# Linear attention with per-channel decay, feed-forward and experts: attention's output made transposed in 32- and 64-column groups of the matmul array, reciprocal decays made by a backward scan

## The chip, the core and the metric

The kernel runs on one core of one Trainium2 chip. The metric is the device time of one launch in microseconds (us); lower is better. Engines are named as in the profile: PE (matmuls), PEld (loads of a matmul's stationary operand), DVE, ACT, POOL, SP (issues most transfers).

## The reference

Three steps follow each other. The first is a recurrence over 768 positions, for 4 batches and 8 heads of 48 channels:

```python
for t in range(S):
    cur = np.einsum('bhd,bhe->bhde', u[None] * kt, vt)
    y[:, :, t] = np.einsum('bhd,bhde->bhe', rt, state + cur)
    state = wt[:, :, :, None] * state + np.einsum('bhd,bhe->bhde', kt, vt)
```

Its output, 3072 tokens by 384, goes through `x @ w_in` (384 to 2048), `max(h, 0) + alpha * min(h, 0)` and `@ w_out` (2048 to 384). The last step routes each token to one of 8 experts (384 to 1024 to 384, relu) by the largest of 8 logits and scales by its probability. All of it is fp32.

## The kernel before

**Stages.** The 3072 tokens are 24 tiles of 128, and 8 blocks of 3 tiles. Attention of tiles 0 to 2 is a prologue. Then the feed-forward step runs block by block, 16 steps of 128 hidden columns each (`p1`, L575, 9 matmuls of 384 columns; `p2`, L602, 9 matmuls of 384 columns). Attention of the next block's tiles is laid between these steps, and so are, in the first block, the conversion of 16 pieces of weights (`wl_stages`, L195, its word operations on DVE) and, one block late, the routing of a finished block (`gate_block`, L462). At the end the expert units run. A product of fp32 numbers in the two feed-forward steps is made from a high and a low part, three matmuls in one pass each. The matmuls of attention are plain fp32: the trace counts two passes for each of them, and one for a transpose.

**One attention tile** (`att_tile`, L265) works on 4 pairs of heads. Channels lie on partitions (0 to 47 the first head of a pair, 64 to 111 the second) and the 128 positions of each pair along the free axis. `scan` (L274) makes the running products of the decays (`ex`, 4 runs of 129). `decay_r` multiplies r by them on POOL. `rec(0)` takes the reciprocal of every fourth product, `rec(1)` fills the three between by multiplying backwards with the decays, `rec(2)` multiplies k; all on DVE. `diag`, `diag_sum` and `diag_v` make `cv`, v scaled by the sum of r, u and k of the position itself. `scores` (L342) makes a 128x128 matrix for each head, on 48 rows of the array, the two heads of a pair on different rows; ACT copies it out and POOL zeroes the part on and above the diagonal. `ktr` and `kv` make the update of the state; `state` adds it on DVE and multiplies by `pm` on POOL; `pm` is made on ACT (`decay`, L336) and has a single buffer. The output is then made in three places:

- `yst` (L398): 4 matmuls, r stationary (128 columns), the state moving (96 columns), into `py`;
- `yav` (L410), in two halves of 4 heads: scores stationary (128 columns), v moving (48 columns), into the same bank;
- `fin` (L422) adds `cv` on DVE into `x`, and `xtr` (L427) transposes `x` in three matmuls into `px`. ACT copies `px` to `xth` (L441), DVE makes `xtl` from the rest (L446). These are the feed-forward step's input, channels on partitions.

**What sets the order.** Tables of slots (`OPS`, and `PRO_OPS`, `PRO_MOVED` for tiles 0 to 2) give each operation of a tile its slot; a feed-forward step is two slots. On PE the order is that of the tables throughout. On DVE, ACT, POOL and SP it is that of the tables in the prologue, and a list scheduler's from there up to the last steps of the feed-forward stage. Each engine works strictly in its order. A tile's `dm` (r, k, decays, channels on partitions) and `tm` (r, k, v, positions on partitions) are loaded by SP, two tiles ahead.

Of the kernel before, what the change touches and what calls it, by code (L numbers as in the profile page):

```python
# [27 lines left out]
PR = 112  # L28
KC = DM // 128
# [44 lines left out]
}  # L74
PRO_NEXT = ("scan", "rec0", "rec1", "k", "r", "rk")
PRO_MOVED = {
# [20 lines left out]
def attention_mlp_moe(ctx, tc, dmaj, tmaj, ub, alpha, w_in, w_out, w_gate, w_gate_b, wexp, out):  # L97
# [23 lines left out]
    def load_tile(i):  # L121
        if i < NB:
            both = wp.tile([128, 1540 + 3 * DM], F32, tag="W", name="both")
            dm, tm = both[:PR, :1540], both[:, 1540:].rearrange("p (c d) -> p c d", c=3)
# [16 lines left out]
    pool.memset(bmask[0:48, :, 0:48], 1.0)  # L141
    pool.memset(bmask[64:112, :, 48:96], 1.0)
# [11 lines left out]
    pool.memset(apat[:, :, 0:1], 1.0)  # L154
    ident = cst.tile([128, 128], F32, name="ident")
# [109 lines left out]
    def att_tile(i, s0):  # L265
# [8 lines left out]
        def scan():  # L274
            dm = dm_t[i]
            ex = ap.tile([PR, NP, 129], F32, tag="ex", name="ex")
            vec.tensor_tensor_scan(
                out=ex.rearrange("p a t -> p (a t)"),
                data0=dm[:, 1024:1540],
                data1=apat.rearrange("p a t -> p (a t)"),  # L280
                initial=0.0,
                op0=ALU.mult,
                op1=ALU.add,
            )
# [3 lines left out]
            cx["v"] = tm_t[i][:, 2, :]  # L288
            cx["rec"] = ap.tile([PR, NP, 128], F32, tag="rec", name="rec", bufs=1)
# [4 lines left out]
        def rec(n):  # L294

            def at4(t, m):
                return t.rearrange("p a (g m) -> p a g m", m=4)[:, :, :, m]

            rc, ex = cx["rec"], cx["ex"][:, :, 1:129]
            if n == 0:  # L300
                vec.reciprocal(out=at4(rc, 3), in_=at4(ex, 3))
            elif n == 1:
                w = dm_t[i][:, 1024:1540].rearrange("p (a t) -> p a t", a=NP)[:, :, 1:129]
                for m in (2, 1, 0):
                    vec.tensor_tensor(out=at4(rc, m), in0=at4(rc, m + 1), in1=at4(w, m + 1), op=ALU.mult)
            else:
                vec.tensor_tensor(out=cx["k"], in0=cx["k"], in1=rc, op=ALU.mult)

        def diag():
            tm = tm_t[i]  # L310
            rk = ap.tile([128, DM], F32, tag="rk", name="rk", bufs=1)
            pool.tensor_tensor(out=rk, in0=tm[:, 0, :], in1=tm[:, 1, :], op=ALU.mult)
            pool.tensor_tensor(out=rk, in0=rk, in1=ub_s, op=ALU.mult)
            cx["rk"] = rk
# [6 lines left out]
        def diag_v():  # L321
            c = cx["c"]
            cv = ap.tile([128, H, D], F32, tag="cv", name="cv", bufs=1)
            if i < NB:
                for h in range(H):
                    act.activation(cv[:, h, :], cx["v"][:, D * h : D * h + D], AF.Copy, scale=c[:, h : h + 1])
            else:
                pool.tensor_tensor(
                    out=cv,
                    in0=cx["v"].rearrange("p (h d) -> p h d", h=H),  # L330
                    in1=c.rearrange("p (h o) -> p h o", o=1).to_broadcast([128, H, D]),
                    op=ALU.mult,
                )
            cx["cv"] = cv
# [63 lines left out]
        def yst():  # L398
            cx["y"] = y_bank("py", [128, DM])
            if not first:  # L400
                for p in range(NP):
                    pe.matmul(
                        cx["y"][:, 96 * p : 96 * p + 96],
                        lhsT=cx["r"][:, p, :],
                        rhs=st_t[i - 1][:, p, :],
                        start=p == 0,
                        stop=False,
                    )

        def yav(g):  # L410
            v = cx["v"]
            for q in range(4):
                h = 4 * g + q
                pe.matmul(
                    cx["y"][:, D * h : D * h + D],
                    lhsT=cx[h % 2][:, h // 2, :],
                    rhs=v[:, D * h : D * h + D],
                    start=first,
                    stop=first or h == H - 1,
                )  # L420

        def fin():  # L422
            x = ap.tile([128, DM], F32, tag="x", name="x", bufs=1)
            vec.tensor_tensor(out=x, in0=cx["y"], in1=cx["cv"].rearrange("p h d -> p (h d)"), op=ALU.add)
            cx["x"] = x

        def xtr():  # L427
# [5 lines left out]
            pa = y_bank("px", [128, KC, 128])  # L433
            for c in range(KC):
                pe.transpose(pa[:, c, :], cx["x"][:, 128 * c : 128 * c + 128], ident)
            cx["px"] = pa
# [6 lines left out]
        def x_low():  # L443
# [5 lines left out]
            "scan": scan, "r": decay_r, "rec0": lambda: rec(0), "rec1": lambda: rec(1), "k": lambda: rec(2),  # L449
            "rk": diag, "c": diag_sum, "cv": diag_v, "sc": scores,  # L450
            "a0": lambda: scores_out(0), "m0": lambda: mask(0), "a1": lambda: scores_out(1), "m1": lambda: mask(1),
            "yst": yst, "yav0": lambda: yav(0), "yav1": lambda: yav(1), "fin": fin, "xtr": xtr, "xh": x_out, "xl": x_low,
# [640 lines left out]
```

## Time and profile before

| what | value |
|---|---|
| runs | 878.28, 880.32, 882.10 us; median 880.32 |
| the profiled execution | 875.71 us, of which span 874.0 us |
| PE busy in the span | 820.5 us (94%) |
| DVE | 645.4 us (74%) |
| ACT | 384.3 us (44%) |
| POOL | 293.4 us (34%) |
| granted TensorE clock, mean | 0.961 of full speed |
| bytes moved | 111.59 MB, mean 128 GB/s |

A busy share is a mean over stages. The first feed-forward matmul starts at 41.8 us, the last piece of weights is converted at about 136 us, the last feed-forward matmuls start at 606 us, and the last matmuls of the experts at 860 us. Busy time by stage is among the rows below. The chain that ended last, as the profile gives it, holds only the last scatter of the output.

### The profile page before, as it was taken

What the parts mean: (1) busy time and instruction counts of PE and PEld (TensorE: products, weight loads), DVE (VectorE), ACT (ScalarE), POOL (GpSimd) and SP (SyncE); (2) the same over time, 40 slices, a digit from 0 to 9 for tenths busy, and PEclk for the clock granted to TensorE, in tenths of its full rate; (3) what the DMA queues carried; (4) which work ended last, traced back from release to release, by engine and by line L of the source; (5) the groups of instructions that cost most, each with busy time, mean ns of one, the idle gap of its engine ahead of it and who ended that gap; (6) DMA issues with size and microseconds to landing.
All of it is one profiled execution on the core that took longest, in us unless ns stands there. A gap on an engine that the chain in (4) does not pass through costs nothing. (4 is left out here: it accounts for less than half of the span.)

```text
span 874.0 us, 14602 instructions
## 1 busy us (share of the span) xinstructions
PE 820.5 (94%) x5453; PEld 796.1 (91%) x5453; DVE 645.4 (74%) x1219; ACT 384.3 (44%) x751; POOL 293.4 (34%) x309
## 2 busy tenths in 40 slices
PE   6878789999799999999999999999999999999994
PEld 4768779999799999999999999999899999999993
DVE  6999898977686996896996983446767576776761
ACT  3545343344133433333333432337355556565641
POOL 5474444233332433343423330122224122232301
PEclk8779888999899999999999999999999999999997
DMA  9625534022212321311312300036456668585830
GB/s 281 203 83 171 193 120 148 29 60 86 59 59 60 87 60 60 86 60 60 86 60 59 87 1 1 28 137 242 147 202 240 224 216 293 204 294 204 275 119 21
DMA packets 30513, 111.59 MB, mean 128 GB/s; under 512 B 8229, under 2 KB 11592, under 8 KB 30440
## 3 DMA queue, kind: packets, MB, share of 16 engines
q1 hardware_dynamic: 26088, 100.38, 35.8%
q0 software_dynamic: 4352, 10.26, 3.2%
q8 instruction: 44, 0.72, 0.3%
q14 instruction: 29, 0.24, 0.1%
HBM read 100.95 MB, written 10.45 MB: 127 GB/s over the span
## 5 line engine op out<-in xcount | busy, mean ns | idle before, releaser
L584 PE MATMUL ph<-xth,wih 128*128 128x384 f32 x384 | 138.1, 360 | 8.4 <-DVE gt L589 5.2
L610 PE MATMUL py<-woh,gh 128*128 128x384 f32 x384 | 138.1, 360 | 1.0 <-ACT gh L595 1.0
L584 PE MATMUL ph<-xth,wil 128*128 128x384 f32 x384 | 132.9, 346 | 6.2 <-DVE wil L229 6.2
L595 ACT CAST gh<-gt 128x384 fp32r<-128x384 f32 x128 | 65.6, 513 | 158.5 <-DVE gt L589 158.5
L610 PE MATMUL py<-woh,gl 128*128 128x384 f32 x384 | 131.4, 342 | 1.4 <-DVE gl L597 1.4
L584 PE MATMUL ph<-xtl,wih 128*128 128x384 f32 x384 | 132.3, 345 | 0.0
L610 PE MATMUL py<-wol,gh 128*128 128x384 f32 x384 | 131.2, 342 | 0.0
L597 DVE TENSOR_TENSOR gl<-gt,gh 128x384 fp32r<-128x384 f32 x128 | 91.9, 718 | 33.3 <-ACT gh L595 31.8
L589 DVE SCALAR_TENSOR_TENSOR gt<-gn,oma_s,ph 128x384 f32<-128x384 f32 x128 | 76.4, 597 | 50.3 <-ACT gn L587 50.1
L587 ACT ACTIVATE gn<-ph 128x384 f32<-128x384 f32 x128 | 62.7, 490 | 113.2 <-PE ph L584 110.1
L815 DVE SCALAR_TENSOR_TENSOR gl<-ph,gh 128x256 fp32r<-128x256 f32 x96 | 40.4, 422 | 73.9 <-ACT gh L813 67.2
L489 DVE SCALAR_TENSOR_TENSOR sink<-x,wgb 128x384 f32<-128x384 f32 x144 | 88.1, 634 | 2.1 <-ACT x L621 1.4
L584 PEld LDWEIGHTS ph<-xth,wih 128*128 128x128 f32 x384 | 74.6, 194 | 10.3 <-DVE gt L589 5.8
L810 PE MATMUL ph<-xh,w1h 128*128 128x256 f32 x288 | 81.5, 283 | 1.2 <-DVE gl L815 1.1
L584 PEld LDWEIGHTS ph<-xth,wil 128*128 128x128 f32 x384 | 74.7, 194 | 7.4 <-DVE wil L229 7.4
L884 POOL DMA_INDIRECT out<-ys,meta x28 | 28.5, 1018 | 156.3 <-ACT ys L881 97.5
L810 PE MATMUL ph<-xl,w1h 128*128 128x256 f32 x288 | 80.8, 281 | 0.0
L810 PE MATMUL ph<-xh,w1l 128*128 128x256 f32 x288 | 80.4, 279 | 0.0
L610 PEld LDWEIGHTS py<-woh,gh 128*128 128x128 f32 x384 | 74.7, 195 | 3.0 <-ACT gh L595 1.3
L610 PEld LDWEIGHTS py<-woh,gl 128*128 128x128 f32 x384 | 74.1, 193 | 2.5 <-DVE gl L597 2.5
L584 PEld LDWEIGHTS ph<-xtl,wih 128*128 128x128 f32 x384 | 74.9, 195 | 0.8 <-DVE xtl L446 0.3
L610 PEld LDWEIGHTS py<-wol,gh 128*128 128x128 f32 x384 | 74.6, 194 | 0.0
(211 smaller groups left out, 1906.4 us busy)
## 6 DMA issues: line engine op xcount, KB each, us to landing
raw<-w SPq DMA_DIRECT2D x64, 768.0 KB
dm<-dmaj SPq DMA_DIRECT2D x21, 673.8 KB
tm<-tmaj SPq DMA_DIRECT2D x21, 576.0 KB
raw<-w_out SPq DMA_DIRECT2D x8, 768.0 KB
raw<-w_in SPq DMA_DIRECT2D x7, 768.0 KB
x2d<-x SPq DMA_DIRECT2D x8, 576.0 KB
both<-tmaj SPq DMA_DIRECT2D x3, 576.0 KB
wgb<-w_gate_b SPq DMA_DIRECT2D x2, 768.0 KB
```

Source lines behind the costliest of these rows:

```text
L489: vec.scalar_tensor_tensor(out=sink, in0=x2[:, j, :], scalar=1.0, in1=wgb_t[h][:, e, :], op0=ALU.mult, op1=ALU.mult, accum_out=cx["l"][:, ...
L584: pe.matmul(ph, lhsT=w, rhs=x[:, c, :], start=k == 0, stop=k == 3 * KC - 1)
L587: act.activation(gn, ph, AF.Relu, scale=-1.0)
L589: vec.scalar_tensor_tensor(out=gt, in0=gn, scalar=oma_s[:, f : f + 1], in1=ph, op0=ALU.mult, op1=ALU.add)
L595: act.copy(gh, gt)
L597: vec.tensor_tensor(out=gl, in0=gt, in1=gh.bitcast(F32), op=ALU.subtract)
L610: pe.matmul(y_t[blk][j], lhsT=g[:, sl], rhs=w, start=f == 0 and m == 0, stop=f == NF1 - 1 and m == 2,)
L810: pe.matmul(ph, lhsT=w, rhs=x, start=k == 0, stop=k == 3 * KC - 1)
L815: vec.scalar_tensor_tensor(out=gl, in0=ph, scalar=0.0, in1=gh.bitcast(F32), op0=ALU.max, op1=ALU.subtract)
L884: pool.indirect_dma_start(out=out, out_offset=bass.IndirectOffsetOnAxis(ap=d["meta"][:, j, 0:1], axis=0), in_=ys, in_offset=None, bounds_c ...
```

## The change

**Output.** `fin` and `xtr` go. `yst` now opens the output's bank `px` itself, already transposed (output channels on partitions, positions along the free axis). It begins with three transposes of `cv` that start the accumulation. Then state and v are the stationary operands and r and the scores move, 128 columns each. The output channels are put in a new order, first 32 channels of every head (two chunks of 128 partitions), then the last 16 of every head (one chunk). So a state matmul fills 64 or 32 partitions, and a v matmul 32. `v` is laid out in that order by the host; for the 16-channel parts it comes a second time, padded with 16 zeros on one side (`vz`), so that two heads of a pair add into one group of 32 partitions. The rows of `w_in` are permuted to match.

**Reciprocals.** `rec(0)` takes the reciprocal of the last product of each run alone (4 of 516 columns) and then runs a scan backwards over the decays, `rec[t] = rec[t+1] * w[t+1] + inj[t]`. `rec(1)` is now the product with k.

**Slots.** Without `fin` and `xtr`, `xh` and `xl` move from slot 9 to slot 8. `diag_v` is on POOL for every tile, in two instructions; for tiles 0 to 2 it was 8 instructions of ACT.

```diff
-    "yst": 5, "yav0": 5, "yav1": 6, "fin": 7, "xtr": 8, "xh": 9, "xl": 9,
+    "yst": 5, "yav0": 5, "yav1": 6, "xh": 8, "xl": 8,
...
+TMW = 3 * DM + 32 * H
+DMW = 2 * 512 + NP * 129 + 1
...
-            dm = ap.tile([PR, 1540], F32, tag="dm", name="dm")
-            tm = ap.tile([128, 3, DM], F32, tag="tm", name="tm")
+            dm = ap.tile([PR, DMW], F32, tag="dm", name="dm")
+            tm = ap.tile([128, TMW], F32, tag="tm", name="tm")
...
-                vec.reciprocal(out=at4(rc, 3), in_=at4(ex, 3))
-            elif n == 1:
-                w = dm_t[i][:, 1024:1540].rearrange("p (a t) -> p a t", a=NP)[:, :, 1:129]
-                for m in (2, 1, 0):
-                    vec.tensor_tensor(out=at4(rc, m), in0=at4(rc, m + 1), in1=at4(w, m + 1), op=ALU.mult)
+                vec.reciprocal(out=inj[:, :, 128], in_=ex[:, :, 128])
+                vec.tensor_tensor_scan(
+                    out=rc.rearrange("p a t -> p (a t)")[:, ::-1],
+                    data0=dm_t[i][:, 1025 : 1025 + NP * 129][:, ::-1],
+                    data1=inj.rearrange("p a t -> p (a t)")[:, ::-1],
+                    initial=0.0, op0=ALU.mult, op1=ALU.add,
+                )
...
-            if i < NB:
-                for h in range(H):
-                    act.activation(cv[:, h, :], cx["v"][:, D * h : D * h + D], AF.Copy, scale=c[:, h : h + 1])
-            else:
+            for at, w, out in ((0, 32, cv[:, : 32 * H]), (64, 16, cv[:, 32 * H :])):
                 pool.tensor_tensor(
...
-                    pe.matmul(
-                        cx["y"][:, 96 * p : 96 * p + 96], lhsT=cx["r"][:, p, :], rhs=st_t[i - 1][:, p, :],
...
+            for c in range(KC):
+                pe.matmul(
+                    y[:, c, :], lhsT=cx["cv"][:, 128 * c : 128 * c + 128], rhs=ident, is_transpose=True,
+                    start=c == 0, stop=False,
+                )
+            if not first:
+                st, r = st_t[i - 1], cx["r"]
+                for p in range(NP):
+                    o = 64 * (p % 2)
+                    pe.matmul(y[o : o + 64, p // 2, :], lhsT=st[:, p, 0:64], rhs=r[:, p, :], start=False, stop=False)
+                for p in range(NP):
+                    o = 32 * p
+                    pe.matmul(y[o : o + 32, 2, :], lhsT=st[:, p, 64:96], rhs=r[:, p, :], start=False, stop=False)
+
+        def yav(g):
+            y, tm = cx["px"], tm_t[i]
+            for h in range(H):
+                at = cx[h % 2][:, h // 2, :]
+                if g == 0:
+                    o, c, n = 32 * (h % 4), h // 4, 2 * DM + 96 * (h // 2) + 32 * (h % 2)
+                else:
+                    o, c, n = 32 * (h // 2), 2, 3 * DM + 32 * h
+                pe.matmul(y[o : o + 32, c, :], lhsT=tm[:, n : n + 32], rhs=at, start=False, stop=g == 1 and h % 2 == 1)
```

Two places of the order in which the instructions stand. First PE, from tile 3's output on, in the first feed-forward block; before (`at` are scores, `st` the state, `dm` holds r, `tm` holds v, `x` is attention's output, `wih`, `wil`, `woh`, `wol` are weights):

```order
L402 MATMUL py<-st,dm 128x96 x4
L414 MATMUL py<-tm,at_539 128x48
L414 MATMUL py<-tm,at_542 128x48
...
L610 MATMUL py_592<-woh_120,gh 128x384
...
L414 MATMUL py<-tm,at_539 128x48
L414 MATMUL py<-tm,at_542 128x48
...
L584 MATMUL ph<-xth,wih_118 128x384
...
L435 MATMUL px<-ident,x 128x128 x3
```

and of the change, the same place, where a fp32 matmul is again one row:

```order
L411 MATMUL px<-ident,cv 128x128 x3
L419 MATMUL px<-dm,st 64x128 x4
L422 MATMUL px<-dm,st 32x128 x4
L432 MATMUL px<-at_541,tm 32x128
L432 MATMUL px<-at_544,tm 32x128
...
L606 MATMUL py_594<-woh_124,gh 128x384
...
L432 MATMUL px<-at_541,tm 32x128
L432 MATMUL px<-at_544,tm 32x128
...
L580 MATMUL ph<-xth,wih_122 128x384
```

The transposes have moved ahead of the state matmuls, so that three visits to the output between feed-forward matmuls have become two; where 4 + 4 + 4 matmuls and 3 transposes stood, 3 transposes and 8 + 8 + 8 matmuls stand.

Second DVE in the prologue, from tile 1's scan to the product with tile 2's k (scans are printed as SCALAR_TENSOR_TENSOR of 516 columns, `both` holds r, k and the decays of a tile). Before:

```order
L277 SCALAR_TENSOR_TENSOR ex<-both,apat 112x516
L301 RECIPROCAL rec<-ex 112x128
L305 TENSOR_TENSOR rec<-rec,both 112x128 x3
L392 TENSOR_TENSOR st<-pv,pm 112x384
L307 TENSOR_TENSOR both<-both,rec 112x512
L424 TENSOR_TENSOR x<-py,cv 128x384
L318 TENSOR_REDUCE c<-rk 128x8
```

and of the change:

```order
L283 SCALAR_TENSOR_TENSOR ex<-both,apat 112x516
L304 RECIPROCAL inj<-ex 112x4
L305 SCALAR_TENSOR_TENSOR rec<-both,inj 112x516
L396 TENSOR_TENSOR st<-pv,pm 112x384
L314 TENSOR_TENSOR both<-both,rec 112x512
L325 TENSOR_REDUCE c<-rk 128x8
```

Four instructions have become two, and the sum into `x` is gone from the queue ahead of the next tile's scan.

## Rows read from the trace of the kernel before

**Rows 1.** By stage: length, busy PE, PEld, DVE, ACT, POOL, granted clock, DMA share, GB/s.

```profile
0.00:42.00 42.00, 31.30 (x199) 24.53 (x199) 34.21 (x43) 17.96 (x52) 21.52 (x31) 0.82 0.84 252
42.00:137.00 95.00, 75.82 (x404) 71.66 (x404) 88.49 (x108) 45.42 (x82) 48.52 (x44) 0.81 0.44 148
137.00:550.00 413.00, 406.94 (x2724) 397.05 (x2724) 322.07 (x743) 148.42 (x342) 144.33 (x163) 0.99 0.21 60
```

**Rows 2.** Groups of DVE instructions, 0 to 137 us: busy us, mean ns, idle before.

```profile
L305 DVE TENSOR_TENSOR rec<-rec,both 112x128 f32<-112x128 f32 x9 | 8.3, 919 | 0.3
L301 DVE RECIPROCAL rec<-ex 112x128 f32<-112x128 f32 x7 | 6.7, 950 | 0.1
L305 DVE TENSOR_TENSOR rec<-rec,dm 112x128 f32<-112x128 f32 x12 | 5.6, 470 | 0.1
L277 DVE TENSOR_TENSOR_SCAN ex<-both,apat 112x516 f32<-112x516 f32 x3 | 3.7, 1228 | 4.8 <-DMA both<-dmaj 4.8
L424 DVE TENSOR_TENSOR x<-py,cv 128x384 f32<-128x384 f32 x6 | 3.2, 540 | 0.3 <-PE py L414 0.2
```

**Rows 3.** Timeline of PE, 0 to 50 us: start, us, instructions, idle before.

```profile
18.22 2.08 PE L348 MATMUL pa<-both 48*128 48x128 f32 x16 [3.82 <-DVE both L307]
...
26.22 1.16 PE L348 MATMUL pa<-both 48*128 48x128 f32 x16 [1.42 <-DVE both L307]
...
33.40 0.55 PE L435 MATMUL px<-ident,x 128*128 128x128 f32 x3 [2.02 <-DVE x L424]
```

**Rows 4.** Waits of PEld, 42 to 137 us: us in total, times, longest.

```profile
PEld ph L584 <- DVE wil L229: 7.4, 3, 5.3
PEld ph L584 <- DVE gt L589: 4.7, 1, 4.7
PEld px L435 <- DVE x L424: 4.6, 2, 3.7
```

**Rows 5.** Timeline of PE: tile 13's state and first v matmuls, and tile 7's scores.

```profile
315.92 0.34 PE L610 MATMUL py<-woh,gl 128*128 128x384 f32 x1
316.10 1.03 PE L402 MATMUL py<-st,dm 112*128 112x96 f32 x8
316.96 1.02 PE L414 MATMUL py<-tm,at 128*128 128x48 f32 x8
...
318.06 0.34 PE L584 MATMUL ph<-xtl,wih 128*128 128x384 f32 x1
...
165.09 0.34 PE L584 MATMUL ph<-xth,wil 128*128 128x384 f32 x1
165.36 1.16 PE L348 MATMUL pa<-dm 48*128 48x128 f32 x16
...
166.73 0.34 PE L610 MATMUL py<-wol,gh 128*128 128x384 f32 x1
```

**Rows 6.** Score matmuls (L348) that run in a stretch after their first start.

```profile
165.37:165.56 0.19, 0.19 (x2) 1.00 0.00 0
```

**Rows 7.** One stretch as in rows 1; timelines of PE, ACT and POOL around 230 us.

```profile
232.07:238.89 6.82, 5.50 (x18) 5.50 (x19) 6.82 (x15) 1.38 (x3) 2.77 (x3) 0.50 0.01 2
...
233.40 0.90 PE L435 MATMUL px<-ident,x 128*128 128x128 f32 x3 [6.06 <-DVE x L424]
...
229.57 0.37 ACT L339 ACTIVATE pm<-bmask,ex 112x96 f32<-112x96 bf16 x1 [11.57 <-POOL st L395]
...
228.40 0.18 POOL L548 COPY g_meta<-tokid 128x3 int32<-128x3 int32 x1 [5.14 <-DMA metad<-g_meta,g_slot]
228.54 0.99 POOL L395 TENSOR_TENSOR st<-st,pm 112x384 f32<-112x384 f32 x1
```

**Rows 8.** Groups of the whole span that price added instructions.

```profile
L549 DVE RECIPROCAL g_meta<-g_se 128x3 f32<-128x3 f32 x8 | 1.4, 178 | 0.2
...
L328 POOL TENSOR_TENSOR cv<-tm,c 128x384 f32<-128x384 f32 x21 | 20.0, 951 | 53.4 <-DVE x L424 51.5 <-DVE c L318 1.9
...
L326 ACT ACTIVATE cv<-both,c 128x48 f32<-128x48 f32 x24 | 5.7, 330 | 0.0
```

More of the change, by code (lines that the diff above doesn't have):

```diff
@@ L122, in load_tile @@
         if i < NB:
-            both = wp.tile([128, 1540 + 3 * DM], F32, tag="W", name="both")
-            dm, tm = both[:PR, :1540], both[:, 1540:].rearrange("p (c d) -> p c d", c=3)
+            both = wp.tile([128, DMW + TMW], F32, tag="W", name="both")
+            dm, tm = both[:PR, :DMW], both[:, DMW:]
             if i == 0:
@@ L140, in attention_mlp_moe @@
     pool.memset(bmask, 0.0)
-    pool.memset(bmask[0:48, :, 0:48], 1.0)
-    pool.memset(bmask[64:112, :, 48:96], 1.0)
+    for n, w, at in ((0, 32, 0), (0, 16, 64), (64, 32, 32), (64, 16, 80)):
+        pool.memset(bmask[n : n + 48, :, at : at + w], 1.0)
     ones = cst.tile([128, 128], BF16, name="ones")
@@ L154, in attention_mlp_moe @@
     pool.memset(apat[:, :, 0:1], 1.0)
+    inj = ap.tile([PR, NP, 129], F32, tag="inj", name="inj", bufs=1)
+    pool.memset(inj, 0.0)
     ident = cst.tile([128, 128], F32, name="ident")
@@ L287, in scan @@
             cx["k"] = dm[:, 512:1024].rearrange("p (a t) -> p a t", a=NP)
-            cx["v"] = tm_t[i][:, 2, :]
-            cx["rec"] = ap.tile([PR, NP, 128], F32, tag="rec", name="rec", bufs=1)
+            cx["v"] = tm_t[i][:, 2 * DM : 3 * DM]
+            cx["rec"] = ap.tile([PR, NP, 129], F32, tag="rec", name="rec", bufs=1)
         def decay_r():
@@ L311, in diag @@
             rk = ap.tile([128, DM], F32, tag="rk", name="rk", bufs=1)
-            pool.tensor_tensor(out=rk, in0=tm[:, 0, :], in1=tm[:, 1, :], op=ALU.mult)
+            pool.tensor_tensor(out=rk, in0=tm[:, 0:DM], in1=tm[:, DM : 2 * DM], op=ALU.mult)
             pool.tensor_tensor(out=rk, in0=rk, in1=ub_s, op=ALU.mult)
@@ L321, in diag_v @@
         def diag_v():
-            c = cx["c"]
-            cv = ap.tile([128, H, D], F32, tag="cv", name="cv", bufs=1)
-            if i < NB:
-                for h in range(H):
-                    act.activation(cv[:, h, :], cx["v"][:, D * h : D * h + D], AF.Copy, scale=c[:, h : h + 1])
-            else:
+            c, v = cx["c"], cx["v"].rearrange("p (a e) -> p a e", a=NP)
+            cv = ap.tile([128, DM], F32, tag="cv", name="cv", bufs=1)
+            for at, w, out in ((0, 32, cv[:, : 32 * H]), (64, 16, cv[:, 32 * H :])):
                 pool.tensor_tensor(
-                    out=cv,
-                    in0=cx["v"].rearrange("p (h d) -> p h d", h=H),
-                    in1=c.rearrange("p (h o) -> p h o", o=1).to_broadcast([128, H, D]),
+                    out=out.rearrange("p (a m e) -> p a m e", a=NP, m=2),
+                    in0=v[:, :, at : at + 2 * w].rearrange("p a (m e) -> p a m e", m=2),
+                    in1=c.rearrange("p (a m o) -> p a m o", a=NP, o=1).to_broadcast([128, NP, 2, w]),
                     op=ALU.mult,
@@ L398, in yst @@
         def yst():
-            cx["y"] = y_bank("py", [128, DM])
-            if not first:
-                for p in range(NP):
-                    pe.matmul(
[L403 to L427, printed above, removed]
             if j == 0:
@@ L1060 @@
         dw[:, sl, :, 1:] = ww[:, j]
-    dmaj[:, :, 1024:] = dw.reshape(NTILE, PR, 516)
+    dmaj[:, :, 1024 : 1024 + NP * 129] = dw.reshape(NTILE, PR, NP * 129)
     def tmj(x):
         return x.transpose(0, 2, 1, 3).reshape(NTILE, 128, DM)
-    tmaj = np.ascontiguousarray(np.stack([tmj(a["r"]), tmj(a["k"]), tmj(a["v"])], axis=2))
+    v = tmj(a["v"]).reshape(NTILE, 128, NP, 2, D)
+    vs = np.concatenate([v[..., :32].reshape(NTILE, 128, NP, 64), v[..., 32:].reshape(NTILE, 128, NP, 32)], axis=3)
+    vz = np.zeros((NTILE, 128, NP, 2, 2, 16), np.float32)
+    for j in range(2):
+        vz[:, :, :, j, j] = v[:, :, :, j, 32:]
+    tmaj = np.concatenate(
+        [tmj(a["r"]), tmj(a["k"]), vs.reshape(NTILE, 128, DM), vz.reshape(NTILE, 128, 32 * H)], axis=2
+    )
+    heads = np.arange(DM).reshape(H, D)
+    rows = np.concatenate([heads[:, :32].reshape(-1), heads[:, 32:].reshape(-1)])
     ub = np.ascontiguousarray(np.broadcast_to(a["u"].reshape(1, DM), (128, DM)))
     alpha = np.ascontiguousarray(a["moe_alpha"].reshape(NF1, 128).T)
-    w_in = np.ascontiguousarray(a["moe_w_in"].reshape(KC, 128, 8, 256).transpose(2, 1, 0, 3)).view(np.int64)
+    w_in = np.ascontiguousarray(a["moe_w_in"][rows].reshape(KC, 128, 8, 256).transpose(2, 1, 0, 3)).view(np.int64)
     w_out = np.ascontiguousarray(a["moe_w_out"].reshape(8, 2, 128, DM).transpose(0, 2, 1, 3)).view(np.int64)
```

24 lines of the change are left out of this document (11 added, 13 removed), and 16 rows, old and new, of tables (OPS, PRO_MOVED, PRO_OPS).

## The prediction, written before the changed kernel was run

> **What bounds the kernel now.** I read busy time by stage first [rows 1]. In the last of the three stretches PE is busy for 406.9 of 413.0 us at nearly the full clock: work added to PE there adds time, and work taken off DVE does not. In the first two, DVE is busy for 34.2 of 42 us and 88.5 of 95, and PE for about three quarters, with a clock of 0.82 and 0.81. So there DVE should be what counts. The groups of DVE [rows 2] show what attention costs it up to 137 us: the reciprocals and the backward products of seven tiles (0 to 6) and the sums into `x` of six (0 to 5). The timeline of PE [rows 3] shows that this is waited for: the scores of tiles 1 and 2 wait for the product with k, which ends that chain, and the transposes of tile 1 wait for `x`. In the second stretch the loads of PE wait for DVE in 7.4 + 4.7 + 4.6 = 16.7 us [rows 4]: for weights, for the hidden layer and for `x`. These are queues on one engine, so any DVE work removed ahead of them should help.
>
> For the third stretch the timeline of PE [rows 5] gives prices. From the last feed-forward matmul before tile 13's output to the second one behind it 318.06 - 315.92 = 2.14 us pass. Two feed-forward matmuls at 0.175 us (0.18 by their starts there) are in it, so the visit costs 1.79 us; it holds 16 passes: **0.112 us for a pass**. The scores' visit costs 166.73 - 165.09 - 0.35 = 1.29 us for 16 passes of 128 columns. In series they would take 1.79; from the start two run at once [rows 6], so they take 8 x 0.112 = 0.90. The other 0.40 us is what changing to half the rows and back costs: **0.20 us for a change** of the array's division.
>
> Once, at 227 us, PE stands still for 6.1 us [rows 7] and then has half the clock for 6.8 us. The rows lead back: PE waits for `x`, DVE for ACT, ACT for 11.6 us at `pm`, whose one buffer POOL's product with the state still reads, and that stands behind transfers of the routing.
>
> **The change, part by part.** My sum is against the profiled execution, 875.7 us (span 874.0); the median of the runs shown is 880.3, so I shift the result by 4.6.
>
> *DVE up to 137 us.* Removed are 8.3 + 5.6 + 6.7 + 3.2 = 23.8 us [rows 2]. Added are seven scans and seven reciprocals of 4 columns. The nearest row for the scan is the forward one, 1.23 us for the same 516 columns; what reading backwards costs no row shows. A bound from above is the product with a step of 4, 0.470 us for 128 columns, which would make 1.9 us; a scan cheaper than the forward one I exclude, since it goes through as many columns. For the reciprocal there is 0.18 us for 3 columns [rows 8]. So 7 x (1.23 + 0.18) = 9.9 us, at most 14.6, and DVE is relieved by 13.9 us, at least 9.2. How much of it reaches the end? At most all. Against it: the chain of tile 1 begins when its data land, and each `tm` is 128 KB larger, three before the first weights, 0.39 MB at 252 GB/s [rows 1], 1.6 us; `diag_v` of tiles 0 to 2 goes from ACT (5.7 us for three tiles) to POOL, at about 1 us a tile [rows 8], in front of POOL's masking of tile 2; and PE has its own work per tile. I take **-10 us**, about 5 in each stretch, with bounds of 0 and -13.9.
>
> *PE, 137 to 550 us.* 18 tiles (6 to 23) make their output here, three of them (6, 12, 18) without a state. Transposes stay three for three. Before, a tile has 8 passes for the state and 16 for v, in series: 24 x 0.112 = 2.69 us, and 1.79 for a tile without a state. Now there are 8 passes 64 columns wide on two groups, 8 that are 32 wide on four, and 2 x 16 that are 32 wide on four; each still moves 128 columns, as the scores' passes do, so I price it alike. If the groups of columns run side by side as the two groups of rows do, that is (4 + 2 + 4 + 4) x 0.112 = 1.57 us. To this come changes of division: into 64, into 32 and back at the first visit, in and back at the second, 5 x 0.20 = 1.0. That is 2.57 against 2.69, and 8 x 0.112 + 4 x 0.20 = 1.70 against 1.79 without a state: 15 x -0.12 + 3 x -0.09 = -2 us. The 87 changes (15 x 5 + 3 x 4) cost 17.4 us of this. At nothing the term would be -19, at twice the price +15; no row separates a change's drain from the load of wider weights. I take **0**, rounded towards the dearer end, and -11 to +7 for half and one and a half times the price.
>
> The scores divide the rows of the array, though [rows 6]; that columns behave alike is the doubtful step, and no row of this kernel shows a matmul on part of the columns. The Trainium skill ("TensorE: Matmul & The Clock Gate", Part 3, measured speedup) reports 2.38 times the speed for three groups of 32 columns. By an estimate from that figure, four groups would give 2.4 to 3.2, a tile some 0.3 to 0.75 us more than I take, and the sum would be -5 to +3 us.
>
> *Edits at nothing.* `cv` is now needed at the front of the first visit instead of by `fin`. POOL waits for nothing before it but the previous tile's `x` [rows 8], so it is made behind the previous tile's output, most of a tile's time (413 us for 18 tiles, 23 us each) ahead. One more POOL instruction per tile lies beside PE. `fin`, reciprocals and products of the other tiles come off a DVE that PE seldom waits for there. The larger `tm` adds a fifth to a DMA share of 0.21. The slots of `xh` and `xl`, one earlier, only add room. If POOL's cover is lost, PE waits with everything behind the transposes. The stall at 227 us has its links unchanged (routing transfer, state, `pm`) [rows 7]; only `x` is gone from its end, where the feed-forward matmuls behind it wait for ACT too. I keep it: 0, or -9.5 if it vanishes (6.1, and half of 6.8).
>
> Sum: -10 + 0 + 0 = **-10 us**, 865.7 on the profiled execution, **870.3** on the median. Its own range, with part of each bound, is 860 to 877.
>
> **The rivals.**
>
> *Two at a time.* Each matmul is two passes. If matmuls never overtake one another, the first pass of the next group can only start beside the second pass of this one, and four groups are worth two. Place: both visits of 18 tiles. Then a tile takes (4 + 4 + 8 + 8) x 0.112 + 1.0 = 3.69 us, +1.0; without a state 16 x 0.112 + 0.8 = 2.59, +0.8: 15 + 2.4 = +17.4, and with -10 from DVE **+7.4, 887.7: slower**. It decides as soon as it costs more than DVE gives back, at 0.56 us a tile. Against it: with two passes in series the first score pass would run alone, and two run already then [rows 6], so passes were exchanged. For it: two groups need only two at a time, and no row shows more. The Trainium skill (same page, Part 3, the mechanism) says that matmuls start and end strictly in program order, without reordering; by that rule this rival would hold, and the scores' rows speak against it.
>
> *One at a time.* Groups of columns share all their rows, and the streams could exclude each other: (8 + 8 + 32) x 0.112 + 1.0 = 6.38 us, +3.69; without a state 3.58 + 0.8 = 4.38, +2.59: +63, and **933**. For it: v's matmuls before, on all rows, are in series at 0.112. Against it: they use all columns too.
>
> *The relief does not arrive.* DMA, POOL or ACT takes DVE's place up to 137 us, PE as forecast: 0, **880**. For it: ACT is busy for half of the second stretch and DMA for 0.84 of the first [rows 1]. Against it: most waits name DVE [rows 3, 4].
>
> *The stall goes as well.* -19.5, **861**, faster. It depends on when routing transfers land, which the change hardly touches.
>
> **How the numbers follow.** A measurement of this kernel tells 0.5%, 4.4 us, from no change. Chances: forecast 0.42, two at a time 0.20, relief absent 0.18, one at a time 0.10, stall gone 0.10. The range reaches from 858, with the stall gone and some of the changes' lower bound, to 891, with two at a time and a little less from DVE; one at a time is left out, and the tails. Faster: 0.39 of the forecast, 0.10, and 0.04 from the rivals near it, 0.53. Slower: 0.16, 0.10 and 0.02 of absent relief, 0.28. Same: 0.19.
>
> **What would show it.** Right: the backward scan at 1.2 to 1.3 us; tile 2's scores near 22 us instead of 26.2; the first feed-forward matmul near 37 us instead of 41.8, the last weights' conversion about 10 us earlier; the two visits of a tile with a state at 0.33 + 1.12 + 0.6 = 2.05 and 0.45 + 0.4 = 0.85 us beside the feed-forward matmuls around them, and PE still busy throughout. The second visit at 1.3 us means two at a time, at 2.2 one at a time. PE idle ahead of the first transposes, with POOL as releaser, would make the part on `cv` wrong; a first feed-forward matmul at 41 us that on DVE.

## The result, and the profile after

The changed kernel takes **884.4 us** (median of 8 runs, 879.28 to 886.76), the kernel before 879.4 (8 runs on the same chip): a ratio of 1.0052, 95% interval 1.0027 to 1.0076. So it is slower by half a per cent, where 870.3 and faster was forecast. The profiled execution took 886.76 us (span 885.1), 11.1 more than that of before; the medians differ by 5.0.

By stage, which answers to [rows 1]:

```profile
0.00:42.00 42.00, 28.14 (x267) 19.50 (x268) 34.19 (x34) 14.33 (x30) 31.60 (x41) 0.87 0.83 267
42.00:137.00 95.00, 73.97 (x500) 66.68 (x499) 81.84 (x103) 44.16 (x82) 55.59 (x50) 0.84 0.45 155
137.00:550.00 413.00, 395.51 (x3045) 363.42 (x3045) 314.02 (x674) 141.94 (x333) 154.16 (x177) 0.98 0.24 65
```

DVE has less to do in the second stretch, but PE is busy for 395.5 us of the third instead of 406.9, and with less of the clock: PE waits there now, as it did only once before.

The added instructions of DVE up to 137 us, for [rows 2] (eight tiles, one of them begun just before the end):

```profile
L305 DVE TENSOR_TENSOR_SCAN rec<-dm,inj 112x516 f32<-112x516 f32 x5 | 9.2, 1837 | 0.0
...
L305 DVE TENSOR_TENSOR_SCAN rec<-both,inj 112x516 f32<-112x516 f32 x3 | 6.5, 2151 | 0.1
L304 DVE RECIPROCAL inj<-ex 112x4 f32<-112x4 f32 x8 | 1.4, 176 | 0.2
```

The reciprocal costs what was forecast, the scan 1.96 us on average (15.7 us for 8) instead of 1.23.

The two visits to a tile's output, on PE's timeline, for [rows 5]:

```profile
335.66 0.34 PE L606 MATMUL py<-woh,gl 128*128 128x384 f32 x1
335.84 0.49 PE L411 MATMUL px<-ident,cv 128*128 128x128 f32 x3
336.25 0.66 PE L419 MATMUL px<-dm,st 112*64 112x128 f32 x8
336.84 0.43 PE L422 MATMUL px<-dm,st 112*32 112x128 f32 x8
337.08 0.62 PE L432 MATMUL px<-at,tm 128*32 128x128 f32 x16
337.64 0.44 PE L580 MATMUL ph<-xth,wih 128*128 128x384 f32 x1
337.92 0.34 PE L580 MATMUL ph<-xtl,wih 128*128 128x384 f32 x1
...
339.14 0.34 PE L580 MATMUL ph<-xth,wil 128*128 128x384 f32 x1
339.40 0.66 PE L432 MATMUL px<-at,tm 128*32 128x128 f32 x16
340.00 0.44 PE L606 MATMUL py<-woh,gh 128*128 128x384 f32 x1
340.28 0.34 PE L606 MATMUL py<-wol,gh 128*128 128x384 f32 x1
```

Reckoned as in the prediction, the first visit costs 337.92 - 335.66 - 0.35 = 1.91 us and the second 340.28 - 339.14 - 0.35 = 0.79, together 2.70; before it was 1.79 + 0.90 + 0.33 = 3.02. Over the 18 tiles PE has 5 us less to do.

What took it back, first at the routing of the third block. PE, then ACT, POOL, SP and DVE of the changed kernel:

```profile
370.01 0.69 PE L580 MATMUL ph<-xth,wih 128*128 128x384 f32 x1 [4.03 <-DVE gt L585]
...
368.56 0.38 ACT L343 ACTIVATE pm<-bmask,ex 112x96 f32<-112x96 bf16 x1 [10.03 <-POOL st L399]
...
350.11 1.03 POOL L547 DMA_INDIRECT metad<-g_meta,g_slot  x1 [2.77 <-DVE g_slot L539]
354.35 0.96 POOL L547 DMA_INDIRECT metad<-g_meta,g_slot  x1 [3.21 <-DMA metad<-g_meta,g_slot]
...
360.96 1.19 POOL L547 DMA_INDIRECT metad<-g_meta,g_slot  x1 [4.41 <-DMA metad<-g_meta,g_slot]
367.39 0.18 POOL L544 COPY g_meta<-tokid 128x3 int32<-128x3 int32 x1 [5.24 <-DMA metad<-g_meta,g_slot]
367.54 0.99 POOL L399 TENSOR_TENSOR st<-st,pm 112x384 f32<-112x384 f32 x1
...
354.68 0.38 SPq L618 DMA_DIRECT2D x2d<-x  x1
359.94 0.33 SPq L137 DMA_DIRECT2D dm<-dmaj  x1
362.80 0.33 SPq L138 DMA_DIRECT2D tm<-tmaj  x1
...
343.40 3.12 DVE L305 TENSOR_TENSOR_SCAN rec<-dm,inj 112x516 f32<-112x516 f32 x1
346.56 1.32 DVE L314 TENSOR_TENSOR dm<-dm,rec 112x512 f32<-112x512 f32 x1
...
348.33 0.17 DVE L534 TENSOR_TENSOR g_rk<-prk,g_oh 128x24 f32<-128x24 f32 x1
```

It is the chain of [rows 7], from the end to its start: PE waits for DVE's `gt`, that for ACT, ACT for 10.03 us at `pm` for POOL's product with the state, and POOL for the landings of the three scatters, each of which waits for the one before it. The second scatter is issued 0.3 us ahead of the store of x2d and takes until 360.96; the third, issued then, takes until 367.39, beside the loads of the next `dm` and `tm` (674 and 704 KB), which follow the store on SP. The same place in the kernel before:

```profile
354.20 0.96 POOL L551 DMA_INDIRECT metad<-g_meta,g_slot  x1 [3.12 <-DMA metad<-g_meta,g_slot]
...
358.06 1.19 POOL L551 DMA_INDIRECT metad<-g_meta,g_slot  x1 [1.06 <-DMA metad<-g_meta,g_slot]
362.40 0.18 POOL L548 COPY g_meta<-tokid 128x3 int32<-128x3 int32 x1 [3.15 <-DMA metad<-g_meta,g_slot]
362.54 1.02 POOL L395 TENSOR_TENSOR st<-st,pm 112x384 f32<-112x384 f32 x1
...
357.05 0.38 SPq L622 DMA_DIRECT2D x2d<-x  x1
...
347.95 0.17 DVE L538 TENSOR_TENSOR g_rk<-prk,g_oh 128x24 f32<-128x24 f32 x1
```

The wait at `pm` was there in the kernel before, too, at the routings of blocks 0, 2 and 4: 11.6, 4.1 and 2.7 us. Only the first was long enough to reach PE. Now it is 15.5, 10.0 and 7.6 us, and PE stands for 7.57 us (until 230.41), 4.03 (until 370.01) and 1.89 + 2.52 us (until 506.28 and 512.22), each with a granted clock of 0.50, the lower of its two levels (1.2 GHz), behind it:

```profile
225.74:235.98 10.24, 5.57 (x17) 5.57 (x18) 6.23 (x19) 2.71 (x8) 2.12 (x5) 0.50 0.00 0
369.10:375.93 6.83, 5.92 (x18) 5.62 (x18) 6.58 (x21) 2.17 (x7) 0.77 (x3) 0.50 0.01 2
512.46:515.87 3.41, 3.41 (x15) 2.97 (x16) 3.41 (x5) 0.64 (x2) 3.33 (x3) 0.50 0.03 7
```

The routings of blocks 1, 3 and 5 have no product with a state behind them (the tile there begins a batch), and no hole.

The second loss lies in the ramp. DVE's timeline, and PE's at the same time:

```profile
53.30 0.55 DVE L325 TENSOR_REDUCE c<-rk 128x8 f32<-128x384 f32 x1 [4.08 <-POOL rk L320]
...
55.10 0.61 DVE L585 SCALAR_TENSOR_TENSOR gt<-gn,oma_s,ph 128x384 f32<-128x384 f32 x1
...
55.76 0.69 PE L580 MATMUL ph<-xth,wih 128*128 128x384 f32 x1 [8.23 <-DVE gt L585]
```

The scheduler now lays tile 4's `c` ahead of the first `gt`; DVE stands at it for 4.08 us, since POOL is not there yet.

Where each kernel stands against the kernel before, in us, at the first feed-forward matmul of blocks 0 to 7 and at PE's last matmul, profiled executions (`e1` to `e8` are the runs of the next section):

```
block                      0     1     2     3     4     5     6     7   last
before (absolute)       41.8 140.3 206.1 280.6 346.6 412.4 478.5 544.2  861.1
changed kernel          -7.0  -4.6  -5.4  -2.2  -1.8  +5.6  +4.8 +10.2  +11.3
e1 change, pm twice     -4.8  -2.4  -3.2  -9.2  -9.5  -9.2 -10.2 -10.7  -10.3
e2 before, pm twice     +0.9  +1.6  +1.6  -6.7  -6.6  -6.4  -6.0  -5.9   -4.2
e3 scan alone           -0.2  -2.0  -0.2  +3.4  +7.4  +9.9 +11.8 +14.3  +17.7
e4 output alone         -4.0  -7.8  -8.5  -9.9 -10.7  -7.9  -8.5  -9.4   -8.7
e7 e4, pm twice         -3.2  -7.5  -7.8 -14.3 -14.8 -15.8 -16.9 -16.7  -13.3
e8 wide tm alone        -0.1  -0.3  -0.3  -1.2  -1.2  -1.2  -1.1  -1.1   -1.3
```

In the second row, block 2 costs +3.2, block 4 +7.4 and block 6 +5.4 us: the three with a routing and a state behind it.

### The profile page after: what moved, and what is told of

Its sections match the earlier page's. It is cut to its first block, busy times and chain, and to the rows that moved or that the text cites. A ratio compares the mean times of both kernels' runs of the same rounds, so it can differ in the third digit from the quotient of the medians.

```text
span 885.1 us, 15643 instructions
## 1 busy us (share of the span) xinstructions
PE 814.5 (92%) x5997; PEld 762.5 (86%) x5997; DVE 635.4 (72%) x1147; ACT 376.4 (43%) x727; POOL 323.4 (37%) x339
## 5 line engine op out<-in xcount | busy, mean ns | idle before, releaser
L593 DVE TENSOR_TENSOR gl<-gt,gh 128x384 fp32r<-128x384 f32 x128 | 84.4, 659 | 31.0 <-ACT gh L591 22.5
L485 DVE SCALAR_TENSOR_TENSOR sink<-x,wgb 128x384 f32<-128x384 f32 x144 | 92.3, 669 | 1.4 <-ACT x L617 1.1
```

What stands on the lines that cost most here:

```text
L485: vec.scalar_tensor_tensor(out=sink, in0=x2[:, j, :], scalar=1.0, in1=wgb_t[h][:, e, :], op0=ALU.mult, op1=ALU.mult, accum_out=cx["l"][:, ...
L593: vec.tensor_tensor(out=gl, in0=gt, in1=gh.bitcast(F32), op=ALU.subtract)
```

## The experiments

Each version was measured beside the kernel before on its own chip, where that took 877.4 to 877.9 us (879.4 beside the changed kernel); what one version is worth against another is taken between their distances from it.

**The buffer of `pm`.** In the changed kernel and in the kernel before:

```diff
-            pm = ap.tile([PR, NP, 96], F32, tag="pm", name="pm", bufs=1)
+            pm = ap.tile([PR, NP, 96], F32, tag="pm", name="pm", bufs=2)
```

> The changed kernel (884.4 us) with two buffers for pm instead of one, nothing else by hand; the scheduler lays ACT, DVE and POOL anew for it. Theory 1: the gain of the change is lost at the routing of blocks 0, 2 and 4, where ACT stands at pm until POOL, behind the three scatters of the routing, has multiplied the state. The holes of PE there are 7.6, 4.0 and 4.4 us and are followed by 10.2, 6.8 and 3.4 us at half the clock, so 16 + 10 = up to 26 us are to be had: 858 to 868 us, no hole of PE over 2 us between 137 and 550 us, pm waiting for POOL's state for less than 2 us. Theory 2 (the larger tm is to blame, wherever it lands): within 3 us of 884. Theory 3 (the new order of DVE and POOL up to 137 us is to blame, the holes at 47.5 and 85 us): within 4 us of 884, as those holes have another cause.

> The kernel before (879.4 us) with two buffers for pm. Theory 1: it loses only the one hole at 227 us, 6.1 us and half of 6.8 us at half the clock: 879.4 - 9.5 = 870 us, so the changed kernel with two buffers is 2 to 12 us ahead of it, and the change is worth what was forecast once this link is gone. Theories 2 and 3: the changed kernel stays behind this one by 5 us or more even then.

Measured: 865.15 us, ratio to before 0.986 (0.984 to 0.989), and 869.37 us, 0.990 (0.987 to 0.992). Theory 1 holds in both. In the changed kernel the wait of ACT for POOL is gone from the waits; `pm` waits for its own input, 3.1 us at most, and the third stretch is at the full clock:

```profile
ACT pm L343 <- DVE ex L283: 27.0, 14, 3.1
...
137.00:550.00 413.00, 409.46 (x3188) 379.81 (x3186) 321.80 (x696) 152.20 (x351) 162.48 (x181) 1.00 0.23 69
```

In the trace of the first, PE, DVE, POOL and SP keep the order of the changed kernel; only ACT's is new. One buffer is worth 18 us in the changed kernel (from 5.0 us behind the kernel before to 12.7 ahead) and 8 in the other. With it the change gains 4 us.

**One part alone.** The kernel before with the backward scan only, and the changed kernel with the old reciprocals:

> The kernel before with the backward scan alone: one reciprocal of 4 columns and a scan of 516 for the reciprocal of 128 and the three products; output and tm as before. DVE is relieved of 8.3 + 5.6 + 6.7 - 7 x 1.39 = 10.9 us up to 137 us. If relief of DVE in the ramp reaches the end (as forecast) 869 to 873 us with the hole of 227 us unchanged; Theory 1 in addition expects that the time comes out wherever the holes at the routings leave it, 869 to 879, and that any missing gain shows as holes at 220, 365 or 505 us. Theory 3 (the ramp's order eats it): 878 or more with the holes between 45 and 137 us.

> The changed kernel with the old reciprocals (every fourth by reciprocal, three products backwards), so the transposed output, vz in tm and cv on POOL alone. DVE is relieved of 3.2 us (the sums into x) up to 137 us, PE of 0.3 us a tile in 18 tiles, 5 us by the visits measured in the changed kernel (1.92 and 0.80 us). Theory 1: 879.4 - 5 - up to 3 = 871 to 875 us where the routings go as before, up to 884 where all three stall as in the changed kernel; the holes tell which. Theory 2 (the larger tm): 884 or more with the loads of tiles in front of late instructions. Theory 3: as before or better up to 137 us, since the queues of DVE are nearly the old ones.

Measured: 889.98 us, 1.0125 (1.010 to 1.015), and 871.31 us, 0.993 (0.991 to 0.996). The output alone behaves as theory 1 has it: its waits at `pm` are 12.2, 6.2 and 3.8 us, and PE stands behind the first two of them, for 4.0 and 2.3 us. The second:

```profile
355.00 0.38 ACT L340 ACTIVATE pm<-bmask,ex 112x96 f32<-112x96 bf16 x1 [6.16 <-POOL st L396]
```

The scan alone, which only takes work off DVE, is the slowest of these four. Its time is one that theory 3 allows (878 or more), but the place is not theory 3's: in the table it has lost nothing up to block 2, and then loses 2 to 4 us in each block. At the block starts `xtl`, on which the block's first step waits, stands behind the scan; DVE, then POOL, around the start of block 2 of that kernel:

```profile
204.58 3.13 DVE L301 TENSOR_TENSOR_SCAN rec<-dm,inj 112x516 f32<-112x516 f32 x1
...
208.14 0.55 DVE L449 TENSOR_TENSOR xtl<-px,xth 128x384 fp32r<-128x384 f32 x1
...
204.46 1.20 POOL L294 TENSOR_TENSOR dm<-dm,ex 112x512 f32<-112x512 f32 x1 [2.03 <-PE px L438]
```

The scan begins 0.12 us after a product of POOL and takes 3.13 us, where a scan beside an idle POOL takes 1.22.

**The link in another place, the order of `c`, and the size of `tm`.** First the scatters of those three routings behind POOL's product with the state, `pm` with one buffer; then the changed kernel with two buffers and tile 4's `c` queued behind the third step's `gt`; then the output alone with two buffers; then the kernel before with 256 more columns in `tm`.

```diff
+                with tc.issue_after(st_i[t0 + 3 * NB].ins) if blk in (0, 2, 4) else ExitStack():
                     for j in range(nt):
                         pool.indirect_dma_start(
```

```diff
+            with tc.issue_after(gt_i[(0, 2)].ins) if i == NB + 1 else ExitStack():
+                cx["c"] = c, vec.tensor_reduce(out=c, in_=cx["rk"].rearrange("p (h d) -> p h d", h=H), axis=AX.X, op=ALU.add)
```

> The changed kernel (884.4 us), pm with its one buffer, but at the routing of blocks 0, 2 and 4 the three scatters of metad are queued on POOL behind the product with the state (and two masks) that stood behind them; nothing else is moved by hand. Theory 1 (POOL holding the state behind its scatters is what ACT, DVE and PE wait for in turn): the three holes go as with two buffers, 860 to 869 us, ACT waits for POOL's state for less than 3 us there. Rival: what helped in the kernel with two buffers was the new order that the scheduler made for it and not the link; then 875 to 885 us here with holes at 223, 366 and 505 us still there.

> The changed kernel with two buffers for pm (865.2 us) and the sum c of tile 4 queued on DVE behind the result of the third feed-forward step instead of in front of the first; nothing else by hand. DVE stood 4.08 us at c there, waiting for POOL, with the first hidden layer (gt) behind it, and PE had a hole of 6.9 us at 49 us. Theory 3 (that order takes back what the start 5 us earlier had gained): 4 us less, 858 to 862 us, the hole at 49 us at 3 us or less. Rival (gt is held up by ACT or the words anyway): 864 to 866 us with a hole of 5 us or more at the same place.

> The transposed output alone (old reciprocals, 871.3 us) with two buffers for pm. Theory 1: it loses its two holes at routings, 4.0 and 2.3 us, and half of 6.8 and 3.4 us at half the clock behind them: 871.3 - 6.3 - 5.1 = 860 us. If that is so, the backward scan is worth nothing beside it: the changed kernel with two buffers has 865.2. If the scan is worth the 5 us of the ramp that the forecast gave it, this kernel comes out at 868 us or more.

> The kernel before (879 us) with the larger tm alone: 256 columns of zeros that nothing reads behind v, 128 KB more a tile; the order on all engines is that of before. Theory 2 (the larger transfer delays the landings of the routing's scatters or the first tiles): 882 to 890 us, the stall at 227 us longer than 6.1 us, or new ones at 360 and 490 us. Theory 1 without it (the order of the instructions around the scatters decides): within 3 us of before, 877 to 882, with the first scores up to 1.6 us later.

Measured:

- State ahead of the scatters: 873.96 us, 0.995 (0.993 to 0.998). 8 us of the 18; the waits at `pm` are 2.7 us at all three. Another wait behind the same scatters is left: `rk` follows them on POOL, and DVE stands at `c`, with `gl` and PE behind it (5.22 us of PE at 232 us).

```profile
236.47 0.55 DVE L325 TENSOR_REDUCE c<-rk 128x8 f32<-128x384 f32 x1 [7.51 <-POOL rk L320]
```

- The late `c`: 862.68 us, 0.982 (0.980 to 0.985), about 2 us less than with two buffers alone, which is little more than the intervals; block 1 starts 6.7 us ahead of before instead of 2.4. That is half of what theory 3 expected, just outside its 858 to 862, and the hole became no smaller: it moved (7.9 us at 45 us), and what was gained lies behind it.
- Output alone with two buffers: **859.50 us**, 0.978 (0.976 to 0.981), the 860 expected. The fastest here, 9.5 us ahead of the kernel before with two buffers, and 5 us ahead of the changed kernel with two buffers: beside the new output the scan, with the order that comes with it, costs time.
- Wide `tm`: 878.29 us, 1.0007 (0.999 to 1.003): no difference. Theory 2 falls.

**Scan and POOL.** In the kernel with the late `c`, and in the one with the scan alone, POOL's products with r and with r and k wait for the scan from tile 4 on:

```diff
+                for p in cx["ri"] if i >= NB + 1 else ():
+                    tc.add_manual_dep(p.ins, cx["bs"].ins.name, mybir.DependencyInfo(
+                        mybir.DependencyClass.Sync, mybir.DependencyReason.DATA), reason="r after scan")
```

> The changed kernel with two buffers for pm and the late c of tile 4 (862.7 us), where from tile 4 on POOL's products with r and with r and k wait for the backward scan on DVE instead of running beside it. In the changed kernel that scan takes 2.12 us on average, 1.22 where POOL is idle and 2.0 to 3.1 where it begins beside a product of POOL. Theory 4 (a scan that begins beside POOL's work stands until that ends): 1.2 to 1.4 us for each scan from tile 4 on, and POOL's first product behind it back at 1.0 from 1.9 us. On the time: 860 to 862 us if the longer scan delayed something that PE waits for (the feed-forward results behind it), 862 to 864 if not. Rival (reading backwards costs more, by the data or the address order): the scans stay at 2 us and more.

> The kernel before with the backward scan alone (890.0 us), with POOL's products waiting for the scan in the same way. There each block begins with a hole of PE of 1.4 to 2.4 us, where xtl stands on DVE behind a scan of 2.2 to 3.1 us. Theory 4: with scans of 1.2 us xtl is ready in time, the five holes of 206, 284, 354, 423 and 491 us go with the half clock behind two of them: 890 - 10.4 - 3.4 = 876 to 880 us. Rival (the holes come from the scheduler's order alone): 887 to 892 us with the holes still there.

Measured: 863.16 us, 0.983 (0.980 to 0.986), and 884.64 us, 1.007 (1.005 to 1.010). The scan, changed kernel first, then with POOL behind it:

```profile
L305 DVE TENSOR_TENSOR_SCAN rec<-dm,inj 112x516 f32<-112x516 f32 x21 | 44.4, 2116 | 0.4
```

```profile
L305 DVE TENSOR_TENSOR_SCAN rec<-dm,inj 112x516 f32<-112x516 f32 x21 | 28.5, 1356 | 0.4
```

Theory 4 holds: beyond 137 us the scans take 1.22 to 1.24 us, but for one of 1.63, so reading backwards costs nothing. It is not what the changed kernel loses time by: 863 is 863. With the scan alone the five holes at the block starts are gone, but a stall at 367 us (4.2 us of PE behind `x`, 8.4 us at `pm`) has come in their place, and 5 of the 10 to 14 us expected arrive.

**The price of columns.** The output alone with two buffers, and 8 matmuls with weights of zero a tile in front of the second visit:

```diff
+            for h in range(H if g == 1 else 0):
+                o = 32 * (h % 4)
+                pe.matmul(y[o : o + 32, 2, :], lhsT=zw, rhs=cx[h % 2][:, h // 2, :], start=False, stop=False)
```

and the same with `o = 0`.

> The transposed output with old reciprocals and two buffers for pm (859.5 us) with 8 more matmuls per tile at the front of the second visit, all with weights of zero, 32 columns wide, spread over the four groups of columns; the sums stay what they were. Two passes each, 16 in all. If groups of columns run side by side (theory of the forecast): 4 x 0.112 = 0.45 us more, the visit 1.25 instead of 0.80 us, and 18 x 0.45 = +8 us beyond 137 us, 867 to 869. Two at a time: 8 x 0.112 = 0.90 us, 1.70 and +16. In series: 1.79 us, 2.59 and +32 us.

> The same 8 more matmuls with weights of zero per tile, all of them in the first group of columns, so that none of them can run beside another. If the groups are what makes them run side by side: 16 x 0.112 = 1.79 us more, the visit 2.59 us, 18 x 1.79 = +32 us, 890 to 893 us. If a pass on 32 columns is simply a quarter of the time: 1.25 us as with the spread ones, and the same time as those.

Measured: 866.67 us and 890.82 us. PE's timeline, spread over four groups, then all in one:

```profile
310.21 0.64 PE L427 MATMUL px<-at,zw 128*32 128x128 f32 x16
310.67 0.66 PE L434 MATMUL px<-at,tm 128*32 128x128 f32 x16
```

```profile
319.82 1.94 PE L427 MATMUL px<-at,zw 128*32 128x128 f32 x16
321.59 0.66 PE L434 MATMUL px<-at,tm 128*32 128x128 f32 x16
```

From start to start 16 passes take 0.46 us in four groups and 1.77 in one: 0.029 and 0.111 us for a pass. Four groups are worth four at a time, and a narrow pass by itself costs what a wide one does.

**Why the waits grew.** Two edits that leave the order of all other instructions as it was on every engine: eight buffers for `g_meta`, so that the copy between the third scatter and the state has nothing to wait for; and the store of x2d made to wait for the third scatter's landing. The loads of `dm` and `tm` that stand behind the store on SP start later with it.

```diff
-            meta = small("meta", I32, 2)
+            meta = mp.tile([128, nt, 2], I32, tag="g_meta", name="g_meta", bufs=NBLK)
```

```diff
+        if 0 < blk < NBLK - 1:
+            tc.add_manual_dep(d.ins, sc_i[blk - 1].ins.name, mybir.DependencyInfo(
+                mybir.DependencyClass.Sync, mybir.DependencyReason.DATA), reason="x2d")
```

> The changed kernel (884.4 us) with a buffer of its own for the meta of each routing (8 instead of 2). The copy of the token numbers for the routing after the next stood on POOL between the third scatter and the product with the state and waited there until that scatter had landed; now all copies stand at the front of the program, and every other instruction keeps its place on all engines. Theory 1: POOL comes to the state when it has issued the third scatter, 6.8, 5.4 and 4.0 us earlier, so the waits at pm shrink from 15.5, 10.0 and 7.6 to about 9, 5 and 4 us; a wait of 4 us made no hole in the kernel before. 868 to 873 us, the holes at 366 and 505 us gone, the one at 223 us at 2 us or less. Rival (the second and third scatter hold POOL as long): 880 to 885.

> The changed kernel with the store of a block's 576 KB (x2d) made to wait until the third scatter of the running routing has landed; the order of the instructions is the same on every engine, and the loads of dm and tm behind the store on SP come later with it. Theory 5 (why the waits at pm grew from 11.6, 4.1 and 2.7 to 15.5, 10.0 and 7.6 us: the store is issued 4.6 us behind the first scatter at the routings of blocks 0, 2 and 4 instead of 6.1 to 7.0, and the second and third scatter land behind its transfers): each scatter then lands in about 4 us, POOL comes to the state 4 to 8 us earlier, holes at 366 and 505 gone, 868 to 875 us. Rival (the scatters are as slow by themselves, or are held up by the loads of dm and tm issued before them): 882 us or more, the waits at pm as long as in the changed kernel.

> The transposed output with old reciprocals and two buffers for pm (859.5 us) and the own buffers for meta as well. With the link at pm gone, POOL's stand behind the scatters reaches PE only by the hole of 1.7 us at 231 us (the sum c of a later tile on DVE): 857.5 to 859.5 us. If that hole has another cause: 859 to 860, no change that can be measured.

Measured:

- Own meta: 876.45 us, 0.998 (0.995 to 1.000). The waits at `pm` are 7.6, 2.7 and 2.7 us, shorter than expected, the holes at 366 and 505 us gone and the one at 223 us 2.5 us long: the link is as theory 1 has it, and 6 us come of it. That is 3 to 8 us short of the expected 868 to 873: this execution starts block 1 2.1 us later than the changed kernel's and has a hole of 2.4 us at 430 us.
- The store behind the scatters: 872.76 us, 0.993 (0.990 to 0.996). The scatters of the third block on POOL:

```profile
342.73 1.03 POOL L547 DMA_INDIRECT metad<-g_meta,g_slot  x1 [1.61 <-DVE g_slot L539]
346.87 1.01 POOL L547 DMA_INDIRECT metad<-g_meta,g_slot  x1 [3.11 <-DMA metad<-g_meta,g_slot]
...
350.90 1.09 POOL L547 DMA_INDIRECT metad<-g_meta,g_slot  x1 [1.18 <-DMA metad<-g_meta,g_slot]
354.98 0.18 POOL L544 COPY g_meta<-tokid 128x3 int32<-128x3 int32 x1 [3.00 <-DMA metad<-g_meta,g_slot]
```

From first scatter to last landing 12.3 us instead of 17.3: theory 5 holds for the store and the loads behind it together; they were moved as one, and the store's part alone is not shown. 10 us come of it. The waits at `pm` are 11.0, 5.0 and 4.3 us, close to before, and only the first reaches PE.
- Best version with own meta: 860.66 us, 0.980 (0.977 to 0.983), no change from 859.5 that can be measured.

## Why the prediction was wrong, step by step

- **The step that failed: "The stall at 227 us has its links unchanged (...). I keep it: 0".** The links were the same, their times were not. A wait of the same kind stood at two more routings, 4.1 and 2.7 us long, and I looked only where PE had stopped. Two buffers give back 18 us in the changed kernel and 8 in the kernel before, so this term was **+9 us** and not 0: without the link the change gains 4 us, with it it loses 5. In the changed kernel DVE comes to `g_rk` 3.5 us behind a block's start instead of 1.3 (348.33 - 344.9 and 347.95 - 346.6), behind a scan of 3.1 us at this place and in a new order (block starts from the table). The first scatter goes out 2 us later, the store of x2d does not, and so lies 4.6 us behind it instead of 7.0 (354.68 - 350.11 and 357.05 - 350.04). The second scatter lands beside the store's 576 KB and the third beside the loads that follow it, and the chain scatter, state, `pm`, `gn`, `gt` carries that to PE. e14 shows that these transfers lengthen the chain, e8 that the larger `tm` by itself does not. Why they cost so much here stays open. The distance alone does not decide it: with the old reciprocals and one buffer (e4) `g_rk` is as late (3.2 to 4.4 us) and the store lies 4.6 to 4.9 us behind the first scatter, yet the waits are 12.2, 6.2 and 3.8 us. Nor is a store beside a scatter always dear: in the kernel before the third scatter, issued 1.0 us behind the store, had landed after 4.3 us (358.06 to 362.40).
- **DVE relief, "-10".** Both halves of it were too large. The 9.9 us of added work were 15 (7 x (1.96 + 0.18)), beyond the 14.6 set as the most. I priced the scan by a forward one that had POOL idle beside it (1.23, right when alone). The trace before had shown the bound's mechanism in its products: 919 ns for some, 470 for others of the same shape [rows 2]. The Trainium skill ("SBUF — State Buffer", who interferes with whom) says that a DVE instruction with two inputs in SBUF, the on-chip memory of the operands, contends with a GpSimd (POOL) instruction that reads SBUF, and calls the ports that the two engines share an exclusive lock; the scans of 2.1 and 3.1 us beside POOL and 1.22 without it agree. Second, relief is not time: the first feed-forward matmul came at 34.7 us, earlier than the 37 forecast and 7.0 before the 41.8 of the kernel before, and of these 7.0 us 4.6 were left at block 1, after DVE had stood at `c`. The other signs fell short too: tile 2's scores came at 24.6 us instead of 22, and the last conversion of weights began 1.3 us earlier (132.8 against 134.1) instead of 10. The kernel with the old reciprocals, with more work on DVE, was at block 1 7.8 us early. Order counted for more than load.
- **PE, "0".** The mechanism was right and the size too small: groups of columns do run four at a time, the visits were forecast at 2.05 and 0.85 us and cost 1.91 and 0.79. With these the term is 15 x -0.32 and 3 x -0.2, **-5 us**. My -2 had a change of division too dear, and the rounding to 0 gave the rest away. Four groups gave 3.8 times (1.77 / 0.46), more than the 2.4 to 3.2 of the estimate. That the 5 us reach the end is not shown: from block 1 to block 7, e1 and e7 are 0.8 and 1.7 us shorter than e2 in the table, one execution each.
- **`cv` and `tm` at nothing** were right: the transposes waited for `cv` 2.3 us in the whole span, and the load alone changed nothing.
- **The rivals.** Two at a time and one at a time are refuted by 0.029 against 0.111 us for a pass. "The relief does not arrive" was near: POOL, one of the engines that it named, is busy for 87.2 us up to 137 us (31.60 + 55.59) instead of 70.0, and `c`, at which DVE stands, waits for it. "The stall goes as well" named the right place with the wrong sign; I did not price that it could grow.

With the link cut, the changed kernel is 12.7 us ahead of the kernel before; the forecast's sum with the stall gone was 19.5 ahead, and of the 6.8 us between them the late `c` gives 2 back.

What stays open: the changed kernel with two buffers and the late `c` (862.7) is 3 us behind the output alone with two buffers (859.5). The scan's length is not the reason (863.2 with short scans); the order of DVE, ACT and POOL differs between the two in many places, and which of them counts was not tried.

## What to carry to other kernels

A wait that is hidden today is a price with a threshold: before an edit is costed at nothing, list all waits of the same kind, the ones too that reach nobody, and how much each may grow before they do. Where one engine waits for a small transfer with other work queued behind it, a second buffer for what that work reads is cheap insurance: here 18 us for 1.5 KB a partition. Removing work from an engine that a scheduler orders anew is worth what the new order makes of it, so measure each part of such a change alone.

## What was not expected of the hardware

- fp32 matmuls on four groups of 32 columns ran four at a time, each with its two passes: 0.029 us for a pass of 128 columns instead of 0.111. Between feed-forward matmuls, which use the whole array, 16 such passes cost 0.79 us and not 0.46.
- A DVE scan with both inputs in SBUF took 1.22 us alone and 2.0 to 3.1 us when it began beside a POOL product. POOL's next product paid too (1.8 to 1.9 instead of 1.0 us).
- A scatter of 128 entries of 8 bytes kept POOL waiting for its landing for 3.0 to 3.3 us where no large transfer was under way (e14; 5.8 us for the first scatter of the first of these routings), and in the changed kernel for up to 6.8 us beside loads of 674 and 704 KB on the other queue.
